# Attention and two expert layers on one core: the load of q, and where its transposes are copied

## The chip, the cores and the metric

The kernel runs on one core of one Trainium2 chip. The metric is the device time of one execution in microseconds. A core has engines that each take their own instructions in the order of the program: TensorE (PE) multiplies, and its weight loads are shown apart (PEld); VectorE (DVE), ScalarE (ACT) and GpSimd (POOL) do elementwise work; SyncE (SP) issues the DMAs here. PE writes to PSUM, the other engines copy from there to SBUF.

## The reference, cut

Attention without softmax comes first, with 8 batches of 8 heads, 576 positions and 64 columns, then two layers of two matmuls each:

```python
def _attn_ref(q, k, v, g_norm):                    # each [8, 8, 576, 64]
    kv = np.einsum('bhsd,bhse->bhde', k, v)
    out = np.einsum('bhsd,bhde->bhse', q, kv)
    rms = np.sqrt(np.mean(out * out, axis=-1, keepdims=True) + 1e-06)
    return (out / rms * g_norm).astype(np.float32)
...
    x = np.ascontiguousarray(attn_out.transpose(0, 2, 1, 3)).reshape(B * S, H * D)   # [4608, 512]
    x = _moe_ref(x=x, **moe_kwargs)       # h = x @ w_in [512, 2048]; max(0.01 h, h) @ w_out [2048, 512]
    return _moe2_ref(x=x, **moe2_kwargs)  # h = x @ w_in [512, 2048]; (h - tanh h) @ w_out [2048, 512]
```

q, k, v and the output are fp32; the four weight matrices come as fp64.

## The kernel before

**The big matmuls.** Each matmul of the two layers is cut into two by two blocks and done with seven products of sums of blocks in place of eight of blocks. Each product is taken from fp16 high and low parts of both operands, in PE instructions of 128x288 (L637). ACT and DVE make the high and low parts of the activations (tiles opa and ops, L574 and L581), POOL and DVE the sums of blocks (L614). A product's result goes from PSUM (ps_a to ps_d) to an SBUF tile u or c by ACT (L694) and is added to the layer's result g by DVE (L705); ACT applies the activation (L1258), and g is stored to DRAM by SP (L784).

**The weights.** A block of a weight matrix comes in as pairs of 32-bit words (L415) and is made into fp32 w1f (L429 on ACT, L433 to L473 on DVE, L496 and L500 on POOL). A maximum over the weights (mw, L465; m_w, L360; most_w, L331) gives a scale, s1g at L375. With it ACT writes the high part (L516) and DVE the low part (L519) of a block w_0, w_1, ... The first layer's columns use w_0 to w_7 in turn.

**Attention.** A batch goes in four pairs of heads; `load_pair` loads k, v and q of one pair. Positions are cut in a way that partition p holds the six positions 6p to 6p+5, so CP = 96 partitions and NC = 6 chunks. k and v come in one DMA each, with 6x64 values in a row of DRAM per partition and head. q comes in two DMAs, one for each head, into a tile laid out as chunk, head, column, in pieces of 64 values. In `pair`, step kv multiplies k by v (L962, PSUM tile pk), and ACT copies the two heads' 64x64 blocks to the diagonal of kvd (L973). Step qtr(r) transposes three chunks of both heads by three PE instructions to one PSUM bank pq (L982); ACT copies its 128x288 to qt[r] (L990), where 64 partitions hold one head and 64 the other. Step o(r) multiplies kvd by qt[r] (L998, PSUM tile po), so o(0) needs the first copy and o(1) the second. ACT squares po (L1004), and ACT (first batch) or DVE (L1013) copies it to xg. Step m sums the squares (L1035, pm); root and reciprocal of this are iv (L1057, L1065). For the first batch PE spreads iv over the partitions (pb, L1102) and DVE multiplies xg by it (L1108); for later batches iv goes through DRAM to a tile bc (L1074) and POOL multiplies (L1080).

**Order.** Class Plan sets the order of all instructions in one run through the program, from durations and delays written by hand: each step is put into the time line of its engine where it fits, and the order of the planned times is the order of the program. A step's planned time thus moves other engines' steps around it. Loads stand on SP in planned order too: in the first 48 us k, v and q of a pair and then four blocks of words; there are never more than eight loads under way, and an issue beyond that waits. The first batch's pairs run before the first product; three pairs of the second batch follow between its first products, and each later pair is spread over products of the stream, its steps kv, qtr(0), qtr(1), o(0), o(1), m at offsets 1, 4, 6, 8, 10 and 13 products. At the end `store` writes the output rows.

Of the kernel before, what the change touches and what calls it, by code (L numbers as in the profile page):

```python
# [11 lines left out]
F32 = mybir.dt.float32  # L12
I32 = mybir.dt.int32
AF = mybir.ActivationFunctionType
# [16 lines left out]
P = 128  # L31
# [170 lines left out]
@with_exitstack  # L202
def body(ctx, tc, *args):
    q, out, w1 = args[0], args[-1], args[4]
    sizes = (*q.shape, *out.shape, w1.shape[1])
    pools = {
        "const": ctx.enter_context(tc.tile_pool(name="const", bufs=1)),
        "wpool": ctx.enter_context(tc.tile_pool(name="wpool", bufs=1)),
        "work": ctx.enter_context(tc.tile_pool(name="work", bufs=1)),
        "dram": ctx.enter_context(tc.tile_pool(name="dram", bufs=1, space=DRAM)),  # L210
        "ps": ctx.enter_context(tc.tile_pool(name="ps", bufs=1, space=PSUM)),
    }
    delays = {}
    unseen = Unseen()
    while True:
        late = lay_out(Plan(delays, True), unseen, {n: unseen for n in pools}, sizes, [unseen] * len(args))
        if late is None:
            break
        delays[late[0]] = delays.get(late[0], 0.0) + late[1]
    with tc.manual_schedule():  # L220
        lay_out(Plan(delays, False), tc.nc, pools, sizes, args)


def lay_out(plan, nc, pools, sizes, args):
    q, k, v, g_norm, w1, w2, w3, w4, out = args
    B, H, S, D, NT, DM, DFF = sizes
    NP = DFF // P // 2
    CP = 96
    NC = S // CP
    T1 = S // 2  # L230
# [9 lines left out]
    L, M, X = (Slots(work, kind, n) for kind, n in (("l", NL), ("m", NM), ("x", NX)))  # L240
# [4 lines left out]
    def bank(n, name):  # L245
        if n in used:
            plan.miss(("bank", n))
        used.add(n)
        return ps.tile([P, 512], F32, tag=f"p{n}", name=name)

    def free(n):
        used.discard(n)
        plan.met(("bank", n))
# [31 lines left out]
    ident = const.tile([P, P], F32, name="ident")  # L285
# [641 lines left out]
    def att_bank(name):  # L927
        n = next(n for n in ATT if n not in used and n != att_n[0])
        att_n[0] = n
        return bank(n, name), n  # L930
# [3 lines left out]

    def load_pair(b, c, held):
        for nm, src in (("k", k), ("v", v), ("q", q)):
            apart = nm != "q"
            held[nm] = L.take([CP, 2, NC, D] if apart else [CP, NC, 2, D], F32, nm)
            if apart:
                nc.sync.dma_start(  # L940
                    out=held[nm].ap.rearrange("p h c d -> p h (c d)"),
                    in_=src[b, 2 * c:2 * c + 2].rearrange("h (p c) d -> p h (c d)", p=CP),
                )
                continue
            for h in range(2):
                nc.sync.dma_start(out=held[nm].ap[:, :, h], in_=src[b, 2 * c + h].rearrange("(p c) d -> p c d", p=CP))

    kv_n = [0]

    def two_heads(t, a):  # L950
        return t.ap[:, a].rearrange("p h d -> p (h d)")

    def pair(b, c, held):

        kk, n = c % 2, c // 2
        qt, sq, po = {}, {}, {}
# [19 lines left out]
                L.give(held["v"])  # L976
            plan.do("A", e + 0.15, 0.5, go)

        def qtr(r):
            qt[r] = att_bank("pq")  # L980
            for a in range(NC // 2):
                nc.tensor.transpose(  # L982
                    qt[r][0][:, CP * a:CP * a + CP], two_heads(held["q"], r * NC // 2 + a), ident[:CP, :CP]
                )

        def q_after(r, e):
            def go():
                src, n_ = qt[r]
                qt[r] = X.take([P, T1], F32, "qt")
                nc.scalar.activation(out=qt[r].ap, in_=src[:, :T1], func=AF.Copy)  # L990
                free(n_)
                if r == 1:
                    L.give(held["q"])
            plan.do("A", e + 0.15, 0.42, go)

        def o(r):
            po[r], po[r, 0] = att_bank("po")
# [161 lines left out]
    t = 1.0  # L1159
# [7 lines left out]
    for o in order:  # L1167
        if o[0] == "a":
            held = {}
            at(t, lambda o=o, held=held: load_pair(o[1], o[2], held))  # L1170
            ta[o[1:]] = (t + 6.5, held)
            t += 3.4
        else:
            later = after_scale.setdefault(o[1:], []) if o[1] in LATE else None
            convert(0, o[1], o[2], t, 5.5, place_w1(o[1], o[2]), later, sums_first(*o[1:]) if o[1] in SOON else [])
            t += 1.7
# [38 lines left out]
    for hp in range(4):  # L1215
        c = PAIRS[hp]
        t_, held = ta[0, c]
# [16 lines left out]
    for b in range(1, B):  # L1234
        for hp in range(4):
            c = PAIRS[hp]
# [3 lines left out]
            held = ta[b, c][1] if (b, c) in ta else {}  # L1240
# [4 lines left out]
    for n, b, c, held in loads:  # L1245
        extra.setdefault(max(n, 0), []).insert(0, (0.0, lambda b=b, c=c, held=held: load_pair(b, c, held), None))
# [199 lines left out]
    e = c3 + 20.0  # L1446
# [6 lines left out]
    def store(t, col0, d0, n):  # L1453

        r = 0
        while r < P:
            b, rest = divmod(col0 + r, S)
            c, p0 = divmod(rest, CP)
            m = min(P - r, CP - p0)
            nc.sync.dma_start(out=out_view[b, c, p0:p0 + m, d0:d0 + n], in_=t[r:r + m, :])  # L1460
            r += m
# [59 lines left out]
```

## Time and profile before

| | us |
|---|---|
| time, median of 3 runs | 1518.28 (1515.27 to 1518.82) |
| time of the profiled execution | 1520.94 |
| span of the profiled execution | 1519.1 |
| PE busy in it | 1452.1 |
| DVE, ACT, POOL busy | 1249.7, 903.6, 673.5 |

The profiled execution is one run that the profiler recorded; its span goes from the first to the last instruction, and its time is 1.8 us longer. An engine's rows have the start of an instruction, its duration, the engine, the line, the operation, the tile written and the tiles read. What stands in brackets behind a row is the time in which the engine stood idle before it, and the instruction or DMA that ended the idle time. Start to start, instructions of an engine lie a little closer than their durations say, since one begins before the one ahead has ended. The granted clock PEclk is a share of 2.4 GHz.

### The profile page before, as it was taken

The page shows a single profiled execution, that of the slowest core. Times are in us where ns is not written, and L with a number is a line of the kernel's source. Part 1 is how long each engine was busy: PE and PEld are TensorE (multiplying, and loading weights), DVE is VectorE, ACT ScalarE, POOL GpSimd, SP SyncE. Part 2 cuts the span into 40 slices and gives each one's busy share as a digit, 9 for nine tenths or more (in the row PEclk, how much of TensorE's full clock was granted, in tenths as well). Part 3 has the DMA queues.
Part 4 walks back from the last instruction along what each step waited for, and adds up shares of the span by engine and source line. Part 5 has one row for each costly group of instructions (what it writes and reads, how often), then busy time and mean ns, then how long its engine had stood idle before and what let it go on. Part 6 is the DMA issues. An engine that isn't in the chain of part 4 may idle for free. (4 is left out here: it accounts for less than half of the span.)

```text
span 1519.1 us, 32831 instructions
## 1 busy us (share of the span) xinstructions
PE 1452.1 (96%) x12674; PEld 1198.8 (79%) x12674; DVE 1249.7 (82%) x1971; ACT 903.6 (59%) x1461; POOL 673.5 (44%) x636
## 2 busy tenths in 40 slices
PE   6589899999999999999999999999998999999998
PEld 3367677776777777777777888888887888888887
DVE  5796677777877899999996888978999988888871
ACT  4477666667767645444442677778877554445540
POOL 3142330353642455445442355458876543444430
PEclk9799999999999999999999999999999999999999
DMA  9937999999977845655555865546668744444431
GB/s 247 205 97 215 260 277 268 265 284 312 325 275 278 333 146 192 202 161 193 186 169 192 318 224 205 210 173 231 244 232 303 248 144 151 144 146 146 142 96 35
DMA packets 187693, 321.82 MB, mean 212 GB/s; under 512 B 54033, under 2 KB 129681, under 8 KB 187537
## 3 DMA queue, kind: packets, MB, share of 16 engines
q1 hardware_dynamic: 187536, 319.73, 66.1%
q8 instruction: 99, 1.62, 0.4%
q14 instruction: 58, 0.47, 0.1%
HBM read 189.66 MB, written 130.01 MB: 210 GB/s over the span
## 5 line engine op out<-in xcount | busy, mean ns | idle before, releaser
L637 PEld LDWEIGHTS <-w 128*128 128x128 f16 x8400 | 821.0, 98 | 218.3 <-issue 42.8
L614 POOL TENSOR_TENSOR gl<-gl 128x256 f32<-128x256 f32 (+1 forms) x272 | 299.5, 1102 | 365.2 <-DVE gl L614 140.1
L637 PE MATMUL ps_a<-ops,w 128*128 128x288 f16 (+1 forms) x2400 | 332.9, 282 | 13.2 <-DVE ops L581 4.8
L637 PE MATMUL ps_c<-ops,w 128*128 128x288 f16 (+1 forms) x2352 | 316.7, 283 | 18.6 <-DVE g L705 18.6
L637 PE MATMUL ps_a<-opa,w 128*128 128x288 f16 (+1 forms) x2016 | 283.8, 281 | 0.1
L637 PEld LDWEIGHTS <-ops 128*128 128x128 f16 x1728 | 169.1, 98 | 20.8 <-issue 1.3
L637 PE MATMUL ps_b<-opa,w 128*128 128x288 f16 (+1 forms) x1200 | 176.0, 283 | 0.0
L614 DVE TENSOR_TENSOR gl<-gl 128x256 f32<-128x256 f32 (+1 forms) x272 | 151.9, 560 | 4.7
L1424 POOL TENSOR_TENSOR g<-g,th 128x512 f32<-128x512 f32 x72 | 113.7, 1579 | 92.9 <-ACT th L1421 85.5
L637 PEld LDWEIGHTS <-opa 128*128 128x128 f16 x1296 | 127.1, 98 | 15.0
L574 ACT ACTIVATE ops<-gl 128x1152 f16<-128x1152 f32 x64 | 74.4, 1162 | 96.5 <-POOL gl L614 96.2
L583 DVE SCALAR_TENSOR_TENSOR ops<-gl,inv,ops 128x1024 f16<-128x1024 f32 x72 | 103.2, 1433 | 29.5 <-ACT ops L576 29.3
L576 ACT ACTIVATE ops<-gl,inv 128x1024 f16<-128x1024 f32 x72 | 82.4, 1144 | 58.5 <-POOL gl L614 58.3
L1080 POOL TENSOR_TENSOR xg<-xg,bc 128x1152 f32<-128x1152 f32 x14 | 37.7, 2694 | 140.3 <-DMA bc<-iv 108.4
L696 ACT ACTIVATE u<-ps_a,up 128x256 f32<-128x256 f32 x144 | 67.9, 472 | 53.5 <-PE ps_a L637 50.0
L705 DVE SCALAR_TENSOR_TENSOR g<-ps_c,u 128x288 f32<-128x288 f32 x128 | 57.8, 452 | 50.7 <-PE ps_c L637 50.1
L581 DVE TENSOR_TENSOR ops<-gl,ops 128x1152 f16<-128x1152 f32 x64 | 93.8, 1470 | 6.2 <-ACT ops L574 6.2
L637 PE MATMUL ps_c<-w,ops 128*128 128x256 f16 x864 | 97.3, 273 | 0.2 <-DVE osb L705 0.2
L637 PE MATMUL ps_a<-w,ops 128*128 128x256 f16 x864 | 95.8, 273 | 0.7 <-ACT c L696 0.7
L614 POOL TENSOR_TENSOR x1g<-x1g 128x256 f32<-128x256 f32 x72 | 66.1, 920 | 48.6 <-DVE opa L583 45.3
L581 DVE TENSOR_TENSOR opa<-gl,opa 128x864 f16<-128x864 f32 x64 | 79.9, 1249 | 3.7 <-ACT opa L574 3.3
L583 DVE SCALAR_TENSOR_TENSOR opa<-gl,inv,opa 128x768 f16<-128x768 f32 x72 | 80.2, 1115 | 0.1
(133 smaller groups left out, 2139.0 us busy)
## 6 DMA issues: line engine op xcount, KB each, us to landing
g<-g SPq DMA_DIRECT2D x64, 576.0 KB, 6.1
gl<-g SPq DMA_DIRECT2D x64, 576.0 KB, 4.5
g<-g SPq DMA_DIRECT2D x72, 512.0 KB, 3.3
gl<-g SPq DMA_DIRECT2D x72, 512.0 KB, 4.3
wd<-wo SPq DMA_DIRECT2D x48, 448.0 KB, 3.4
w<-wd SPq DMA_DIRECT2D x24, 896.0 KB, 7.1
words<-in_moe_w_in_dram SPq DMA_DIRECT2D x64, 256.0 KB, 6.9
words<-in_moe_w_out_dram SPq DMA_DIRECT2D x64, 256.0 KB, 4.7
```

Source lines behind the costliest of these rows:

```text
L574: nc.scalar.activation(out=o, in_=i_, func=AF.Copy)
L576: nc.scalar.activation(out=o, in_=i_, func=AF.Identity, scale=scale())
L581: nc.vector.tensor_tensor(out=o, in0=i_, in1=h, op=ALU.subtract)
L583: nc.vector.scalar_tensor_tensor(out=o, in0=i_, scalar=scale(), in1=h, op0=ALU.mult, op1=ALU.subtract)
L614: lambda: e.tensor_tensor(out=g()[:, o], in0=g()[:, a], in1=g()[:, b], op=op),
L637: nc.tensor.matmul(out=out_, lhsT=a, rhs=c, start=start and m == 0, stop=stop and m == n - 1, skip_group_check=not fresh,)
L696: nc.scalar.activation(out=t, in_=src, func=AF.Identity, scale=self.scale)
L705: nc.vector.scalar_tensor_tensor(out=o, in0=src, scalar=self.minus if sub else self.scale, in1=t, op0=ALU.mult, op1=ALU.add,)
L1080: e.tensor_tensor(out=x, in0=x, in1=held[kk].ap[:, n0:n1], op=ALU.mult)
L1424: e.tensor_tensor(out=g()[:, n], in0=g()[:, n], in1=held["t"].ap[:, n], op=ALU.subtract)
```

## The change

q is loaded as k and v are, in one DMA with 6x64 values in a row. Step qtr takes a head h in place of half of the chunks: each of its three PE instructions transposes two neighbouring chunks of that head together, so partitions 0 to 63 of PSUM hold the even chunks and 64 to 127 the odd ones. Two ACT copies of 64x288 follow: the PSUM half r goes to the head's half of qt[r]. A pair so has four copies in place of two, planned at 0.41 us each, and o(0) needs the first and the third of them, o(1) the second and the fourth. qt[0] now holds chunks 0, 2, 4 and qt[1] chunks 1, 3, 5, and `store` maps the output rows to match. Lines behind the edit carry numbers that are three to eight lower.

```diff
     def load_pair(b, c, held):
         for nm, src in (("k", k), ("v", v), ("q", q)):
-            apart = nm != "q"
-            held[nm] = L.take([CP, 2, NC, D] if apart else [CP, NC, 2, D], F32, nm)
-            if apart:
-                nc.sync.dma_start(
-                    out=held[nm].ap.rearrange("p h c d -> p h (c d)"),
-                    in_=src[b, 2 * c:2 * c + 2].rearrange("h (p c) d -> p h (c d)", p=CP),
-                )
-                continue
-            for h in range(2):
-                nc.sync.dma_start(out=held[nm].ap[:, :, h], in_=src[b, 2 * c + h].rearrange("(p c) d -> p c d", p=CP))
+            held[nm] = L.take([CP, 2, NC, D], F32, nm)
+            nc.sync.dma_start(
+                out=held[nm].ap.rearrange("p h c d -> p h (c d)"),
+                in_=src[b, 2 * c:2 * c + 2].rearrange("h (p c) d -> p h (c d)", p=CP),
+            )
...
-        def qtr(r):
-            qt[r] = att_bank("pq")
+        def qtr(h):
+            held["pq", h] = att_bank("pq")
             for a in range(NC // 2):
                 nc.tensor.transpose(
-                    qt[r][0][:, CP * a:CP * a + CP], two_heads(held["q"], r * NC // 2 + a), ident[:CP, :CP]
+                    held["pq", h][0][:, CP * a:CP * a + CP],
+                    held["q"].ap[:, h, 2 * a:2 * a + 2].rearrange("p c d -> p (c d)"), ident[:CP, :CP],
                 )
 
-        def q_after(r, e):
-            def go():
-                src, n_ = qt[r]
-                qt[r] = X.take([P, T1], F32, "qt")
-                nc.scalar.activation(out=qt[r].ap, in_=src[:, :T1], func=AF.Copy)
-                free(n_)
+        def q_after(h, e):
+            def go(r):
+                src, n_ = held["pq", h]
+                if r not in qt:
+                    qt[r] = X.take([P, T1], F32, "qt")
+                nc.scalar.activation(
+                    out=qt[r].ap[D * h:D * h + D], in_=src[D * r:D * r + D, :T1], func=AF.Copy
+                )
                 if r == 1:
-                    L.give(held["q"])
-            plan.do("A", e + 0.15, 0.42, go)
+                    free(n_)
+                    if h == 1:
+                        L.give(held["q"])
+            plan.do("A", plan.do("A", e + 0.15, 0.41, lambda: go(0)), 0.41, lambda: go(1))
...
-            c, p0 = divmod(rest, CP)
+            n_, p0 = divmod(rest, CP)
+            c = 2 * n_ - (NC - 1) * (2 * n_ // NC)
```

The plan's order moves with the edit. On DVE, from the first batch's scaling to the maximum of the first weights (m_w): L1108 (L1105 after) multiplies xg by the spread norm, L1013 (L1010) copies a pair's output of the second batch, the others convert words. Before:

```order
L1108 TENSOR_TENSOR xg<-xg,pb 128x288
L465 TENSOR_REDUCE mw<-words 128x1
L452 SCALAR_TENSOR_TENSOR w1f_615<-words,w1f_615 128x512
L1108 TENSOR_TENSOR xg<-xg,pb 128x288
L465 TENSOR_REDUCE mw<-words 128x1
L1013 COPY xg<-po 128x288
L360 TENSOR_REDUCE m_w_727<-mw 128x1
```

and after:

```order
L465 TENSOR_REDUCE mw<-words 128x1
L1010 COPY xg<-po 128x288
L446 SCALAR_TENSOR_TENSOR w1f_615<-words,w1f_615 128x512
L1010 COPY xg<-po 128x288
L452 SCALAR_TENSOR_TENSOR w1f_615<-words,w1f_615 128x512
L1105 TENSOR_TENSOR xg<-xg,pb 128x288 x4
L452 SCALAR_TENSOR_TENSOR w1f_615<-words,w1f_615 128x512
L1105 TENSOR_TENSOR xg<-xg,pb 128x288
L360 TENSOR_REDUCE m_w_778<-mw 128x1
```

Between the last maximum over words (mw) and m_w there now stand two copies, three conversions and five multiplications, where one copy stood.

Also on DVE, ahead of the first product that uses w_5: L519 makes the low parts of w_5 and w_6, L705 adds products to g, L446 and L452 convert words. Before:

```order
L705 SCALAR_TENSOR_TENSOR g<-ps_c,u_1133 128x288
L519 SCALAR_TENSOR_TENSOR w_5_1125<-w1f_933,s1g,w_5_1125 128x896
L1013 COPY xg<-po 128x288
L452 SCALAR_TENSOR_TENSOR w1f_1068<-words,w1f_1068 128x512
L705 SCALAR_TENSOR_TENSOR g<-ps_c,u_1296 128x288
L519 SCALAR_TENSOR_TENSOR w_5_1125<-w1f_943,s1g,w_5_1125 128x896
L705 SCALAR_TENSOR_TENSOR g<-ps_b,c_1277 128x288
L519 SCALAR_TENSOR_TENSOR w_6_1242<-w1f_951,s1g,w_6_1242 128x896
L705 SCALAR_TENSOR_TENSOR g<-ps_c,u_1234 128x288
```

and after:

```order
L705 SCALAR_TENSOR_TENSOR g<-ps_b,c_1263 128x288
L473 TENSOR_SCALAR w1f_1159<-w1f_1159 128x512
L446 SCALAR_TENSOR_TENSOR w1f_1159<-words,w1f_1159 128x512
L440 TENSOR_SCALAR w1f_1160<-w1f_1160 128x512
L452 SCALAR_TENSOR_TENSOR w1f_1159<-words,w1f_1159 128x512
L705 SCALAR_TENSOR_TENSOR g<-ps_c,u_1224 128x288
L446 SCALAR_TENSOR_TENSOR w1f_1160<-words,w1f_1160 128x512
L519 SCALAR_TENSOR_TENSOR w_5_1185<-w1f_941,s1g,w_5_1185 128x896
L452 SCALAR_TENSOR_TENSOR w1f_1160<-words,w1f_1160 128x512
L519 SCALAR_TENSOR_TENSOR w_5_1185<-w1f_976,s1g,w_5_1185 128x896
L519 SCALAR_TENSOR_TENSOR w_6_1344<-w1f_1062,s1g,w_6_1344 128x896
```

The add of u_1224 is the one of u_1234 before, that of the last product with w_3, and PE's next product is the first with w_5; both low parts of w_5 now stand behind this add.

On ACT, one of the first pairs that are spread over products: L990 (L984) copies transposes, L694 copies products, L1004 (L1001) squares po. Before:

```order
L990 ACTIVATE qt<-pq 128x288
L694 ACTIVATE c_1682<-ps_a 128x288
L694 ACTIVATE u_1688<-ps_a 128x288
L990 ACTIVATE qt<-pq 128x288
L1258 ACTIVATE g<-g 128x1152
L1004 ACTIVATE sq<-po 128x288
```

and after:

```order
L984 ACTIVATE qt<-pq 64x288 x2
L694 ACTIVATE c_1694<-ps_a 128x288
L694 ACTIVATE u_1700<-ps_a 128x288
L984 ACTIVATE qt<-pq 64x288 x2
L1255 ACTIVATE g<-g 128x1152
L1001 ACTIVATE sq<-po 128x288
```

Two copies stand where one stood, and the rest of the order is the same.

## Rows read from the trace of the kernel before

**Rows 1.** the page, part 1: busy time, share of the span, instructions.

```profile
PE 1452.1 (96%) x12674; PEld 1198.8 (79%) x12674; DVE 1249.7 (82%) x1971; ACT 903.6 (59%) x1461; POOL 673.5 (44%) x636
```

**Rows 2.** waits of PE: line waited for, us in total, times, longest.

```profile
PE ps_c L637 <- DVE g L705: 18.6, 16, 3.0
PE pk L962 <- DMA v<-in_v_dram: 15.4, 6, 6.7
```

**Rows 3.** timeline of PE, the last wait of the start.

```profile
80.56 0.64 PE L637 MATMUL ps_a<-ops,w 128*128 128x288 f16 x2 [2.65 <-DVE ops L581]
```

**Rows 4.** timeline of PE, 164 to 177 us.

```profile
168.42 0.90 PE L637 MATMUL ps_a<-ops,w 128*128 128x288 f16 x6 [3.12 <-ACT u L694]
172.27 1.60 PE L637 MATMUL ps_c<-ops,w 128*128 128x288 f16 x6 [2.71 <-DVE g L705]
```

**Rows 5.** timeline of SP, the loads of one pair, and the next k.

```profile
14.53 0.60 SPq L940 DMA_DIRECT2D k<-in_k_dram  x1
16.04 1.32 SPq L946 DMA_DIRECT2D q<-in_q_dram  x2
17.40 4.86 SPq L415 DMA_DIRECT2D words<-in_moe_w_in_dram  x4
22.30 0.60 SPq L940 DMA_DIRECT2D k<-in_k_dram  x1
```

**Rows 6.** windows: busy time by engine, then clock, DMA share, GB/s; words alone.

```profile
32.00:39.00 7.00, 5.35 (x27) 2.54 (x23) 4.51 (x11) 5.33 (x12) 2.81 (x5) 1.00 1.09 347
```

**Rows 7.** DMA view, 14 to 32 us: GB/s in 40 equal slices.

```profile
GB/s 203 202 228 313 332 346 344 358 337 203 208 242 213 197 214 191 207 211 205 231 319 339 332 351 359 295 217 208 215 225 217 233 171 190 207 180 221 250 290 300
```

**Rows 8.** timeline of DVE: first batch's reciprocal, and the first weight scale.

```profile
46.41 1.94 DVE L1065 RECIPROCAL iv<-iv 128x288 f32<-128x288 f32 x1
63.48 0.15 DVE L375 TENSOR_TENSOR s1g<-s_w,gcol 128x1 f32<-128x1 f32 x1
```

**Rows 9.** timelines of DVE around w_5, and of PE at its first use.

```profile
103.69 1.14 DVE L519 SCALAR_TENSOR_TENSOR w<-w1f,s1g,w 128x896 f16<-128x896 f32 x1
105.11 0.68 DVE L452 SCALAR_TENSOR_TENSOR w1f<-words,w1f 128x512 int32<-128x512 int32 x1
105.71 0.45 DVE L705 SCALAR_TENSOR_TENSOR g<-ps_c,u 128x288 f32<-128x288 f32 x1
106.08 1.66 DVE L519 SCALAR_TENSOR_TENSOR w<-w1f,s1g,w 128x896 f16<-128x896 f32 x1
109.47 0.46 DVE L705 SCALAR_TENSOR_TENSOR g<-ps_c,u 128x288 f32<-128x288 f32 x1 [0.30 <-PE ps_c L637]
...
109.27 0.90 PE L637 MATMUL ps_a<-opa,w 128*128 128x288 f16 x6
```

**Rows 10.** windows (columns as in rows 6), behind the wait at 168 us.

```profile
170.00:177.00 7.00, 4.73 (x21) 3.15 (x21) 6.96 (x11) 4.23 (x8) 5.26 (x5) 0.51 0.75 225
```

**Rows 11.** timelines of SP and POOL, third batch: q's issues, the multiplication by bc.

```profile
153.41 1.37 SPq L946 DMA_DIRECT2D q<-in_q_dram  x2
...
164.50 2.61 POOL L1080 TENSOR_TENSOR xg<-xg,bc 128x1152 f32<-128x1152 f32 x1 [6.75 <-DMA bc<-iv]
```

**Rows 12.** timeline of PE: two later waits in the stream.

```profile
354.44 1.60 PE L637 MATMUL ps_c<-ops,w 128*128 128x288 f16 x6 [1.51 <-DVE g L705]
...
394.41 0.92 PE L962 MATMUL pk<-v,k 96*64 96x64 f32 x24 [1.42 <-DMA v<-in_v_dram]
```

**Rows 13.** groups of ACT by form, 100 to 450 us: busy, mean ns, idle.

```profile
L990 ACT ACTIVATE qt<-pq 128x288 f32<-128x288 f32 x47 | 19.1, 405 | 6.0 <-PE pq L982 6.0
L973 ACT ACTIVATE kvd<-pk 64x64 f32<-64x64 f32 x46 | 9.9, 216 | 7.3 <-PE pk L962 6.9
```

**Rows 14.** timelines of ACT and PE, a streamed pair: second copy, first product.

```profile
99.94 0.41 ACT L990 ACTIVATE qt<-pq 128x288 f32<-128x288 f32 x1 [0.33 <-PE pq L982]
...
101.22 0.65 PE L998 MATMUL po<-qt,kvd 128*128 128x288 f32 x2
```

**Rows 15.** timeline of ACT: the latest copy of the stream's pairs.

```profile
343.51 0.39 ACT L990 ACTIVATE qt<-pq 128x288 f32<-128x288 f32 x1
```

More of the change, by code (lines that the diff above doesn't have):

```diff
@@ L936, in load_pair @@
         for nm, src in (("k", k), ("v", v), ("q", q)):
-            apart = nm != "q"
-            held[nm] = L.take([CP, 2, NC, D] if apart else [CP, NC, 2, D], F32, nm)
-            if apart:
-                nc.sync.dma_start(
-                    out=held[nm].ap.rearrange("p h c d -> p h (c d)"),
-                    in_=src[b, 2 * c:2 * c + 2].rearrange("h (p c) d -> p h (c d)", p=CP),
-                )
-                continue
-            for h in range(2):
-                nc.sync.dma_start(out=held[nm].ap[:, :, h], in_=src[b, 2 * c + h].rearrange("(p c) d -> p c d", p=CP))
+            held[nm] = L.take([CP, 2, NC, D], F32, nm)
[3 more added lines that the diff above has]
+            )
     kv_n = [0]
-    def two_heads(t, a):
-        return t.ap[:, a].rearrange("p h d -> p (h d)")
     def pair(b, c, held):
```

## The prediction, made before the changed kernel was run

> **What bounds the kernel now.** I read the page first. TensorE (PE) is busy for 1452.1 of 1519.1 us [rows 1], and the changed kernel gives it the same matmuls and six transposes per pair of heads as before. So the change can move the time by the 67 us in which PE stands, by PE's clock, and by nothing else. The waits by engine say what PE stands for [rows 2]: 18.6 us for the sums that VectorE (DVE) adds, 15.4 us for v of the attention pairs. PE's times then place them: most of its waits lie before 80.56 us, where the last of the start ends after 2.65 us [rows 3], and the longest later stretch with waits begins at 168.42 us [rows 4]. I therefore take four places apart: the start, the first columns after it, the stalls in the stream, and the transposes themselves.
>
> **Start: q in long rows.** Until 48 us the load queue is the limit: SyncE issues k, v, two halves of q and four blocks of weight words per pair and is held up at the words. From one k to the next it takes 7.8 us (14.53 to 22.30) [rows 5]. A pair brings 0.885 MB of k, v, q and 1.049 MB of words. Words alone move at 347 GB/s [rows 6]; at this rate the 1.93 MB would take 5.6 us. The 2.2 us above that is the most that q's 256-byte rows can cost. The least: the rate falls to about 211 GB/s in the slices with k, v and q and is near 340 between them [rows 7]. If k and v stay at the low rate and q alone rises to 347, its 0.295 MB fall from 1.40 to 0.85 us, a gain of 0.55. Nothing in the slices sets q apart from k and v, which had long rows already, yet q has two transfers and six times as many rows. I take 1.3 us per pair, near the middle.
>
> Four pairs of the first batch stand ahead of the reciprocal at 46.41 us [rows 8], so it comes 5.2 us earlier (2.2 to 8.8). The weight scale s1g at 63.48 gains less: the changed order puts five multiplications, three conversions and a copy more ahead of its maximum on DVE, some 4 us of work of which a part fills DVE's waits; I take half of the gain, 2.6. DVE then makes the operands of the first products ahead of weight splits that stood before them now (two of 1.14 us [rows 9] ahead of the last), and the last operand wait, which ends at 80.56 [rows 3], should so end about 5.3 us earlier. **Start: -5.3** (-2.5 to -8).
>
> **The first columns: a weight that comes late.** The order on DVE shows a cost there. Now the two splits of w_5 run at 103.69 and 106.08, and the second is done at 107.74, 1.5 us before PE needs it at 109.27. The next add, at 109.47, waits for the product just before [rows 9]. In the changed order both splits stand behind that add, with two steps of weight conversion among them. From start to start the rows have 0.37 for an add and 0.60 for a conversion, 0.08 less than they last. So 109.47 plus an add (0.37), a conversion (0.60), a split (1.14 less 0.08), a conversion (0.60) and a split to its end (1.14) gives 113.24. PE could do three matmuls with the first half (0.37), so it stands 3.6 us. DVE can't go ahead: it takes its instructions in the order shown. **+3.6.** After a wait of 3.12 us in the stream the clock was 0.51 for 7 us with 4.73 us of work [rows 4, 10], that is about 1.2 instead of 2.4 GHz, which cost 2.4 us. I take the same here: **+2.4** (0 to 3.4).
>
> **The stall at 168 us.** The third batch's row scales bc are issued right behind q's 153.41, land so late that GpSimd (POOL) waited 6.75 us for them to 164.50, and PE's wait of 3.12 us follows through the operand made from them [rows 4, 11]. The change puts one issue of q in place of two: a k took 0.60 to issue where q's two took 1.32 [rows 5], so SyncE saves some 0.7 us here too, of 1.37 [rows 11], and the transfer some 0.5 to 1.3. Part of the gain is eaten by what is queued beside it: **-1.4** (0 to -5.8 if both waits at 168 and 172 vanish, and 2.4 more if the clock stays up).
>
> **The other stalls in the stream.** One wait for v, 1.42 us at 394.41, ends at a transfer behind q's of the pairs before [rows 12]; with half of q's rate penalty gone I count it out: **-1.4** (0 to -1.9 with a smaller one before it). The wait at 354.44 (1.51 us, with a half clock behind it) [rows 12] comes from an operand behind a stored tile; queues are emptier by a transfer or two: **-1.0** (0 to -3.5).
>
> **The copies.** Before, one ScalarE (ACT) copy of 128x288 filled one qt, 0.405 us each [rows 13]. Now a copy fills 64 of 128 partitions; a copy of half as many partitions with the same 288 columns is nowhere in the trace. The nearest are this one (0.405) and the copy of 64x64 (0.216) [rows 13]. The half copy shares its columns with the first and its partitions with the second; I take 0.41, by the columns, and 0.22 as the low end. 64 more copies are 26 us of ACT, which is busy for 59% of the span [rows 1], so ACT is not the bound. What counts is the order: out product 0 now needs the third copy, the first of the second head, and not the first alone. The transposes of the second part end about 0.03 before ACT takes up the copy at 99.94 and the product starts at 101.22 [rows 14]: ACT may answer 0.86 us late before PE waits. In the 24 pairs of the stream the copy after the second transposes came later than this in three: by 2.04 us at 343.51, where ACT stood behind a weight split that had waited for POOL [rows 15], and by about 0.2 at two others. **+2.4** (0 to +14, the second rival). In the first batch the four copies stand one behind the other ahead of the product; two more of them cost PE 0.6 to 0.8 us per pair, covered by the wait for the next v there, since PE is idle until it comes. If loads get fast enough to remove that cover, that is the price for each of the four pairs. The stores of the last stage are as many as before, to other rows of the output; I cost them at nothing, as they are off PE's path, and 0.5 at worst if the last one is slower.
>
> **Sum.** -5.3 + 3.6 + 2.4 - 1.4 - 1.4 - 1.0 + 2.4 = -0.7 us against the profiled execution. That one took 1520.94, its span 1519.1 and 1.8 around it, and so lies 2.66 above the median of the runs, 1518.28. 1520.94 - 0.7 = 1520.2, less 2.66 is **1517.6**. The bound of a measurement is 0.3%, 4.55 us: faster means below 1513.7, slower above 1522.8. The forecast is thus no change that can be told, with the gain of the loads spent at w_5.
>
> **Rivals.** First, *the loads gain the whole 2.2 us and the stalls go*. Start -8.0, w_5 +3.6 with no loss of clock, the stall at 168 gone with its half clock (-8.2), v -1.9, 354 -2.5, copies +2.4: -14.6, that is 1503.7. For it speaks that words alone reach 347 GB/s and that the stall hangs on a DMA of the queue which gets shorter; against it that k and v in long rows show the low rate as well. Half-way cases lie about 1510.
>
> Second, *ACT becomes the gate of the out products*. Place: the third copy before each first out product; it decides from 0.86 us after the second transposes on. If the added copies, which now also stand in front of the u and c copies of the main products, make ACT late by 0.6 more than its slack in half of the 24 pairs, PE waits 7.2 us, and if three of these waits drop the clock (2.4 each, as in the row of the half clock) 7.2 more: +14.4 in place of +2.4, so 1529.6. For it: ACT's copies come in clumps, and three pairs exceed the slack already. Against it: most of them start 0.15 us after the transposes.
>
> Third, *long rows don't do what they should*: the low rate in the slices belongs to k, v and q alike, whatever the row. Then the start gains nothing, w_5 still costs 3.6 and 2.4, the copies 2.4, and the stall at 168 gives back its 0.7 of issue: +7.7, that is 1526.0. For it speaks that the slices with k and v are as slow as those with q [rows 7]; against it that the stretch of words alone, in long rows, has nearly twice their rate [rows 6]. The Trainium skill's page "DMA: Bandwidth & Descriptors", section "Why small descriptors are slow (HBM only)", gives a packet about 3 cycles above its 32-byte beats, which makes 11 cycles of 256 B. By that (an estimate from the page) q's 66 cycles for six rows become 51, some 0.3 us per pair, and the rival would be off by 1.2. The fall from 347 to about 211 GB/s is larger than that rule gives.
>
> **How the numbers follow.** Forecast .45 (from 1513 to 1522; .38 of it within the bound, .05 faster, .02 slower). First rival .27, all faster, spread from 1503.7 to 1513. Second .15, third .13, both slower. So faster .32, same .38, slower .30. For 8 in 10 I leave out the far half of the second rival and the far third of the first: 1507 to 1528.
>
> **What would show it.** Right: 32 issues of q with 288 KB, the reciprocal about 5 us earlier; a wait of 3 to 4 us for w in the first product of the fifth column, a clock near 0.5 behind it; the stall after the third batch's scales shorter, not gone. The first rival shows as no stall at all there, and a reciprocal 8 us earlier; the second as many waits of out products for the ACT copy of qt, the third as an unchanged distance between two loads of k. I would be wrong most simply if w_5 were in time, or if some other operand were to wait in its place.

## The result, and the profile after

The changed kernel takes 1530.25 us (median, 1522.61 to 1539.89) where the kernel before takes 1517.7 beside it: a ratio of 1.009, with a 95% interval of 1.0065 to 1.0115. It is slower, by 12.6 us between the medians, and outside the range of 1507 to 1528 that was given. Its executions also differ more from each other than those of before (1515.27 to 1519.44). Its profiled execution took 1535.21, 14.3 more than that of before.

The page of the changed kernel, to be read against [rows 1]:

```profile
span 1533.4 us, 32882 instructions
PE 1453.1 (95%) x12674; PEld 1198.9 (78%) x12674; DVE 1252.5 (82%) x1971; ACT 930.0 (61%) x1525; POOL 671.1 (44%) x636
```

PE has the work that it had (1453.1 against 1452.1); ACT has 64 more instructions and 26.4 us more, as worked out. The span is 14.3 us longer, so what was added is PE's waiting, and the clock. The waits of PE by releaser (total us, times, longest), against [rows 2]:

```profile
PE pk L954 <- DMA v<-in_v_dram: 10.5, 3, 7.0
PE ps_a L637 <- ACT u L694: 10.3, 4, 5.2
PE ps_a L637 <- DVE w L519: 8.8, 3, 3.6
PE po L995 <- ACT qt L984: 5.6, 7, 1.1
PE ps_a L637 <- ACT w L516: 1.2, 1, 1.2
```

The waits for v fell from 15.4 to 10.5. That is not the faster load by itself: in the runs below the load alone has 15.1 us of these waits, and the copies with the old load have 10.1, since PE waits for half copies in their place. New are 8.8 and 1.2 us for w, the weights; 5.6 for qt, the half copies; and 6.9 more for u, against this row of before:

```profile
PE ps_a L637 <- ACT u L694: 3.4, 2, 3.1
```

Where on the line of time? The start of each PE instruction of L637 was set against that of the same instruction before (they come in the same order). The difference, in us, runs like this; a minus means that the changed kernel is ahead:

| place (us before) | what changes there | difference behind it |
|---|---|---|
| 84 | start: loads faster, half copies in the way | -3.7 |
| 109 to 123 | first product with w_5 | +8.4 |
| 168 to 323 | stall at bc | +9.4 |
| 323 to 358 | smaller waits gone, 354 with its half clock among them | +4.1 |
| 389 to 395 | wait for v gone | +3.6 |
| 397 to 400 | a new wait | +11.6 |
| 406 | a wait of before gone | +10.2 |
| 424 to 450 | longer waits for DVE's adds | +14.1 |
| the end | | +14.3 |

Two places make most of the loss: 12.1 us at w_5 and 8.0 near 397. A third, between 424 and 450, adds 3.9. PE's timeline at them, with the stall after the third batch's scales in its place:

```profile
106.94 0.42 PE L637 MATMUL ps_a<-opa,w 128*128 128x288 f16 x2 [1.17 <-ACT w L516]
110.93 0.90 PE L637 MATMUL ps_a<-opa,w 128*128 128x288 f16 x3 [3.56 <-DVE w L519]
115.47 0.42 PE L637 MATMUL ps_a<-opa,w 128*128 128x288 f16 x1 [3.65 <-DVE w L519]
...
177.69 0.90 PE L637 MATMUL ps_a<-ops,w 128*128 128x288 f16 x6 [3.95 <-ACT u L694]
...
405.76 1.60 PE L637 MATMUL ps_a<-ops,w 128*128 128x288 f16 x6 [5.24 <-ACT u L694]
...
459.14 1.60 PE L637 MATMUL ps_c<-ops,w 128*128 128x288 f16 x6 [2.58 <-DVE g L705]
```

The first three rows are the first product of w_5: 1.17 + 3.56 + 3.65 = 8.38 us, for ACT's high part and for DVE's two low parts. The fourth answers to [rows 4] and is 0.8 longer than it was. The fifth is new, and the last is 1.5 us longer than before.

The loads at the start did what was expected of them. SyncE's issues of k and words (SP), the 40 slices of GB/s from 14 to 32 us, and the reciprocal on DVE, for [rows 5, 7, 8]:

```profile
11.30 0.32 SPq L938 DMA_DIRECT2D k<-in_k_dram  x1
14.67 2.66 SPq L415 DMA_DIRECT2D words<-in_moe_w_in_dram  x4
17.96 0.32 SPq L938 DMA_DIRECT2D k<-in_k_dram  x1
...
GB/s 296 351 348 346 351 353 322 229 249 246 266 259 248 252 246 305 357 341 353 348 354 298 225 293 225 249 256 245 242 245 307 304 335 350 344 351 348 346 353 341
...
42.73 1.94 DVE L1062 RECIPROCAL iv<-iv 128x288 f32<-128x288 f32 x1
```

From one k to the next it is 6.7 us in place of 7.8, and the slices between the words now lie near 250 GB/s in place of 211. The reciprocal starts at 42.73, 3.7 us earlier.

### The profile page after: what moved, and what is told of

Its sections match the earlier page's. It is cut to its first block, busy times and chain, and to the rows that moved or that the text cites. A ratio compares the mean times of both kernels' runs of the same rounds, so it can differ in the third digit from the quotient of the medians.

```text
span 1533.4 us, 32882 instructions
## 1 busy us (share of the span) xinstructions
PE 1453.1 (95%) x12674; PEld 1198.9 (78%) x12674; DVE 1252.5 (82%) x1971; ACT 930.0 (61%) x1525; POOL 671.1 (44%) x636
## 5 line engine op out<-in xcount | busy, mean ns | idle before, releaser
L637 PEld LDWEIGHTS <-w 128*128 128x128 f16 x8400 | 822.4, 98 | 236.8 <-issue 48.3
L637 PE MATMUL ps_a<-ops,w 128*128 128x288 f16 (+1 forms) x2400 | 333.4, 283 | 17.2 <-ACT u L694 10.3
L637 PE MATMUL ps_c<-ops,w 128*128 128x288 f16 (+1 forms) x2352 | 317.3, 283 | 18.9 <-DVE g L705 18.7
L637 PE MATMUL ps_a<-opa,w 128*128 128x288 f16 (+1 forms) x2016 | 285.8, 282 | 10.1 <-DVE w L519 8.8
L637 PEld LDWEIGHTS <-ops 128*128 128x128 f16 x1728 | 169.1, 98 | 22.0 <-issue 2.5
L637 PE MATMUL ps_b<-opa,w 128*128 128x288 f16 (+1 forms) x1200 | 177.5, 285 | 0.0
L637 PEld LDWEIGHTS <-opa 128*128 128x128 f16 x1296 | 126.8, 98 | 14.7
L705 DVE SCALAR_TENSOR_TENSOR g<-ps_c,u 128x288 f32<-128x288 f32 x128 | 57.9, 452 | 49.6 <-PE ps_c L637 48.6
L637 PE MATMUL ps_a<-w,ops 128*128 128x256 f16 x864 | 95.8, 273 | 1.9 <-ACT c L696 1.9
L637 PE MATMUL ps_c<-w,ops 128*128 128x256 f16 x864 | 97.3, 273 | 0.2 <-DVE osb L705 0.2
```

The lines of the kernel that those rows point to most:

```text
L637: nc.tensor.matmul(out=out_, lhsT=a, rhs=c, start=start and m == 0, stop=stop and m == n - 1, skip_group_check=not fresh,)
L705: nc.vector.scalar_tensor_tensor(out=o, in0=src, scalar=self.minus if sub else self.scale, in1=t, op0=ALU.mult, op1=ALU.add,)
```

## What happens at w_5

The prediction read the order of DVE right and the time wrong. DVE and POOL of the changed kernel at that place, and behind them two windows (busy time by engine, then granted clock, DMA share, GB/s):

```profile
107.37 3.50 DVE L519 SCALAR_TENSOR_TENSOR w<-w1f,s1g,w 128x896 f16<-128x896 f32 x1
110.79 3.09 DVE L452 SCALAR_TENSOR_TENSOR w1f<-words,w1f 128x512 int32<-128x512 int32 x1
113.81 4.40 DVE L519 SCALAR_TENSOR_TENSOR w<-w1f,s1g,w 128x896 f16<-128x896 f32 x3
...
106.95 6.38 POOL L1077 TENSOR_TENSOR xg<-xg,bc 128x1152 f32<-128x1152 f32 x2 [1.36 <-ACT w L516]
...
111.00:115.50 4.50, 0.85 (x4) 0.24 (x5) 4.50 (x3) 0.00 (x0) 4.50 (x3) 0.50 0.85 226
115.50:122.00 6.50, 6.50 (x31) 4.52 (x32) 4.18 (x6) 3.90 (x7) 3.85 (x5) 0.58 0.02 4
```

The two splits of w_5 stand where the order shows them. But the first lasts 3.50 us where [rows 9] has 1.14, and the conversion behind it 3.09 where it had 0.68. From 106.95 to 113.3 GpSimd runs the second batch's two multiplications by bc: 6.6 us of DVE's time stand beside them, for 1.8 us of work. In the kernel before, they began only after both splits were done:

```profile
110.98 5.43 POOL L1080 TENSOR_TENSOR xg<-xg,bc 128x1152 f32<-128x1152 f32 x2 [1.49 <-ACT qt L990]
```

The windows behind the waits show about half the clock, 0.50 with 0.85 us of PE's work and 0.58 with 6.50. At the full clock that work takes 0.4 and 2.7 us less: most of the 3.7 us that the 12.1 have above the waits.

The trace of before has the same thing, where it cost nothing. An add and a conversion on DVE, and the multiplication on POOL beside them:

```profile
268.06 0.46 DVE L705 SCALAR_TENSOR_TENSOR g<-ps_b,c 128x288 f32<-128x288 f32 x1
268.43 3.11 DVE L446 SCALAR_TENSOR_TENSOR unit<-words,unit 128x512 int32<-128x512 int32 x1
...
268.36 2.63 POOL L1080 TENSOR_TENSOR xg<-xg,bc 128x1152 f32<-128x1152 f32 x1 [0.93 <-PE pq L982]
```

The add of 0.46 us begins shortly ahead; the conversion, 0.68 us alone, lasts 3.11: it ends 0.55 us after GpSimd's 2.63 are over. It is so for every conversion and split with two SBUF inputs that began more than 0.05 us behind such a multiplication and before its end, in this trace and in that of the changed kernel: a conversion ended 0.55 us behind the multiplication's end, a split 0.95 to 0.97. Those that began ahead of it kept their 0.68 and 1.14. The Trainium skill, page "SBUF — State Buffer", section "Who interferes with whom", states this as a rule: a VectorE instruction with two SBUF inputs and a GpSimd instruction that reads SBUF exclude each other for the whole of the instruction. The traces agree: what reads PSUM as one input (L705, L1013) keeps its 0.46 us beside GpSimd, what reads two SBUF tiles (L446, L519) does not when it begins second. A conversion with one SBUF input (L440, 0.43 us alone) didn't keep its time either: 1.35 to 2.62 us in the trace of before.

## Experiments

Each kernel was measured on one chip together with the kernel before, and its ratio is to that. Three kernels part load, copies and order. The plan's order follows from planned durations alone, so each can be changed without the others.

**The load alone**: the kernel before, with the changed `load_pair`, and

```diff
 def two_heads(t, a):
-    return t.ap[:, a].rearrange("p h d -> p (h d)")
+    return t.ap.rearrange("p h c d -> p (h c d)")[:, 2 * D * a:2 * D * a + 2 * D]
```

> The changed load alone: q in one DMA with rows of 1536 B. Transposes, copies and the order on TensorE, VectorE, ScalarE and GpSimd are those of before; since the transposes take q's tile as it lies, heads and chunks are mixed and the output is not the reference's. Theory O (the order that the plan made of the change costs the time, at w_5 above all): the gain of the start stays, first operand wait over 3 to 5 us earlier, no wait for w near 109 us, no half clock there; 3 to 6 us faster than before, about 1513. Theory C (more copies on ScalarE cost the time): the same here, so this run doesn't part O from C. Theory L (the long rows themselves make other transfers land late, as the operand that waited 8.6 us for a DMA near 404 us in the changed kernel): a stall of over 3 us in the stream that before doesn't have, 1520 or more.

Measured: 1512.83 us, ratio 0.9968 (0.9956 to 0.998), a gain of 4.9 us. PE at the end of the start, at the stall after bc, at the wait of 354 us and at a wait for v:

```profile
76.13 0.64 PE L637 MATMUL ps_a<-ops,w 128*128 128x288 f16 x2 [2.65 <-DVE ops L581]
...
163.51 0.90 PE L637 MATMUL ps_a<-ops,w 128*128 128x288 f16 x6 [2.59 <-ACT u L694]
...
348.56 0.90 PE L637 MATMUL ps_c<-ops,w 128*128 128x288 f16 x6 [0.86 <-DVE g L705]
...
389.07 0.92 PE L957 MATMUL pk<-v,k 96*64 96x64 f32 x24 [2.98 <-DMA v<-in_v_dram]
```

The start is 4.4 us earlier ([rows 3]), and of the stalls in the stream little is gained on balance: the one at 168 us is 0.5 shorter, the wait at 354 is 0.65 shorter and PE has its full clock behind it (1.00, against 0.57 before), which makes 2.3, and the wait for v at 394 is 1.6 longer than in [rows 12]. No new stall: theory L falls, and nearly all of the load's gain is what the start gives, 1.1 us per pair.

**Copies and order alone**, with the load of before: the changed kernel with the old `load_pair` and

```diff
-                    held["q"].ap[:, h, 2 * a:2 * a + 2].rearrange("p c d -> p (c d)"), ident[:CP, :CP],
+                    two_heads(held["q"], h * (NC // 2) + a), ident[:CP, :CP],
```

> The load of before (two DMAs per pair in 256-byte pieces) with the changed transposes, the four half copies and the changed order on all engines; q's tile is read in another order than it was loaded, so heads and chunks are mixed and the output is not the reference's. Theory O: the changed kernel without the gain of the start (3.7 us before w_5), so 1530 to 1536, with the waits for w_5 (over 7 us together) in the profile. Theory C: the same. Theory L: the stall near 404 us goes, about 1520 to 1525.

Measured: 1536.72 us, ratio 1.0121 (1.0108 to 1.0134). PE waits 8.22 us at w_5, and 5.79 at 407.79 for u, behind the same wait of ACT as below. Without the faster load the loss is larger.

**The changed kernel in the order of before**:

```diff
-            plan.do("A", plan.do("A", e + 0.15, 0.41, lambda: go(0)), 0.41, lambda: go(1))
+            plan.do("A", plan.do("A", e + 0.15, 0.21, lambda: go(0)), 0.21, lambda: go(1))
```

> The changed kernel with each half copy planned at 0.21 us in place of 0.41: the plan then gives TensorE, VectorE and GpSimd the order of before, row for row, and ScalarE too, but for two half copies in each copy's place. All the work of the changed kernel is in it. Theory O: no wait at w_5 and no half clock there; the start 3 to 5 us earlier than before, some 1 to 4 us of waits of out products for the half copies in the stream: 1513 to 1519. Theory C: ScalarE's 26 us more cost the same as in the changed kernel, 1527 or more. Theory L: as in the first run, with a new stall in the stream, 1520 or more.

Measured: 1518.66 us, ratio 1.0001 (0.9991 to 1.0011). It does all the work of the changed kernel and is as fast as before. So by these ratios the load gives 4.9 us, the half copies take 5.0, and the order that the plan makes of 0.41 us takes the rest, 10.6 to 13.5 (the changed kernel was measured twice, at 1.0071 below and at 1.009). The 4.9 and 5.0 belong to the order of before; in the changed order the load gives 4.7 to 7.6 by the ratios, and what the copies take there was not measured. Theory O holds for the larger part and C for 5 us. PE's waits for the copies at the start, with ACT beside one of them, the one wait in the stream, and two of SyncE's issues of k:

```profile
19.37 2.29 PE L995 MATMUL po<-qt,kvd 128*128 128x288 f32 x4 [1.28 <-ACT qt L984]
27.30 1.24 PE L995 MATMUL po<-qt,kvd 128*128 128x288 f32 x4 [1.40 <-ACT qt L984]
...
17.52 0.82 ACT L984 ACTIVATE qt<-pq 64x288 f32<-64x288 f32 x2 [0.23 <-PE pq L974]
18.24 0.65 ACT L429 ACTIVATE w1f<-words 128x512 f32<-128x512 f32 x1
18.91 0.83 ACT L984 ACTIVATE qt<-pq 64x288 f32<-64x288 f32 x2
...
345.01 0.75 PE L995 MATMUL po<-qt,kvd 128*128 128x288 f32 x2 [2.05 <-ACT qt L984]
...
13.06 0.32 SPq L938 DMA_DIRECT2D k<-in_k_dram  x1
20.88 0.32 SPq L938 DMA_DIRECT2D k<-in_k_dram  x1
```

In the first batch each first out product waits 0.9 to 1.4 us for its third copy, and ACT shows why: a conversion of words (L429) stands between the two pairs of copies. The first product of L637 starts at 72.71 where the load alone has 66.42. Not all of these 6.3 us need be the copies': from one k to the next it is 7.8 us in this execution, as with short rows, where the load alone has 6.5 (11.04 to 17.57) and the changed kernel 6.7. Why the long rows were no faster here is open, and with it where the 5.0 us stand. In the stream the one long wait is 2.05 us, at the pair of [rows 15], where 2.04 was forecast.

**Who holds up DVE at w_5.** GpSimd's multiplication for the second batch was left out in one kernel:

```diff
-            e.tensor_tensor(out=x, in0=x, in1=held[kk].ap[:, n0:n1], op=ALU.mult)
+            if b != 1:
+                e.tensor_tensor(out=x, in0=x, in1=held[kk].ap[:, n0:n1], op=ALU.mult)
```

> The changed kernel, leaving out GpSimd's two multiplications of the second batch by its row scales (so that batch's rows are not normed); the order of all else is unchanged. They ran beside VectorE's split of w_5 and the conversion behind it, which lasted 3.50 and 3.09 us. Theory P (VectorE's instructions that read two SBUF operands stand while such a GpSimd instruction runs, and this made 3.6 us of expected wait into 8.4): the split lasts about 1.14 and the conversion 0.68, TensorE's waits for w_5 fall from 8.4 to about 4, and the time by 4 to 7 us, to 1523 to 1526. Rival Q (the split lasts long because of its own operands or a late DMA): durations and time unchanged within 2 us.

Measured: 1528.84 us, ratio 1.007 (1.0057 to 1.0083). DVE and PE at w_5:

```profile
107.00 1.14 DVE L519 SCALAR_TENSOR_TENSOR w<-w1f,s1g,w 128x896 f16<-128x896 f32 x1
108.06 0.68 DVE L452 SCALAR_TENSOR_TENSOR w1f<-words,w1f 128x512 int32<-128x512 int32 x1
108.66 3.94 DVE L519 SCALAR_TENSOR_TENSOR w<-w1f,s1g,w 128x896 f16<-128x896 f32 x3
...
106.18 0.42 PE L637 MATMUL ps_a<-opa,w 128*128 128x288 f16 x2 [1.17 <-ACT w L516]
108.19 0.54 PE L637 MATMUL ps_a<-opa,w 128*128 128x288 f16 x3 [1.59 <-DVE w L519]
109.86 0.42 PE L637 MATMUL ps_a<-opa,w 128*128 128x288 f16 x1 [1.12 <-DVE w L519]
```

The split is back at 1.14 and the conversion at 0.68, and PE waits 1.17 + 1.59 + 1.12 = 3.88 us in place of 8.38: P holds at the place, and 3.6 was close for the order by itself. With the clock, PE falls back by 6.2 us at w_5 in place of 12.1. The whole gained little, and the 4 to 7 us that P forecast did not come: the profiled execution is 8.4 us shorter than the changed kernel's, but it is the fastest of its runs, and the ratio of 1.007 is that of the changed kernel's second measurement (1.0071). What took the local gain back in the other runs is not settled.

In another kernel all of these multiplications were cut in four:

```diff
-            x = xg[b, kk].ap[:, n0:n1]
-            e.tensor_tensor(out=x, in0=x, in1=held[kk].ap[:, n0:n1], op=ALU.mult)
+            for m_ in range(n0, n1):
+                e.tensor_tensor(
+                    out=xg[b, kk].ap[:, m_:m_ + 1], in0=xg[b, kk].ap[:, m_:m_ + 1], in1=held[kk].ap[:, m_:m_ + 1],
+                    op=ALU.mult,
+                )
```

> The changed kernel with each of GpSimd's multiplications by the row scales (128x1152) cut into four instructions of 128x288, in the same place of the order. Theory P1 (VectorE waits for the end of the one GpSimd instruction that runs): the split of w_5 and the conversion behind it get in between the pieces and last at most 0.7 us longer than alone, so the waits for w_5 fall from 8.4 to 5 or 6 us and the time by 3 to 5. Rival P2 (VectorE gets no turn as long as GpSimd has work of this kind queued): the split lasts 3 us as before, the time within 2 us.

Measured: 1524.51 us, ratio 1.0035 (1.0022 to 1.0048), against 1.0071 of the changed kernel on the same chip: 5.5 us faster by the ratios. DVE and PE at w_5:

```profile
106.25 1.68 DVE L519 SCALAR_TENSOR_TENSOR w<-w1f,s1g,w 128x896 f16<-128x896 f32 x1
107.86 1.28 DVE L452 SCALAR_TENSOR_TENSOR w1f<-words,w1f 128x512 int32<-128x512 int32 x1
...
105.83 0.42 PE L637 MATMUL ps_a<-opa,w 128*128 128x288 f16 x2 [1.17 <-ACT w L516]
107.99 0.54 PE L637 MATMUL ps_a<-opa,w 128*128 128x288 f16 x3 [1.74 <-DVE w L519]
110.80 0.42 PE L637 MATMUL ps_a<-opa,w 128*128 128x288 f16 x1 [2.27 <-DVE w L519]
```

The split lasts 1.68, the conversion 1.28, PE waits 5.18 us. DVE gets its turn between the pieces: P1 holds, P2 falls. At w_5 PE now falls back by 8.6 us, where the two profiles of the changed kernel have 12.1 and 11.0; so only 2.4 to 3.5 of the 5.5 us stand there, and where the rest comes from was not followed up.

**The stall near 397 us.** The changed kernel once more:

> The changed kernel once more, as the measure for the three beside it on the same chip. Expected 1526 to 1534. If the stall near 404 us belongs to the order that the plan made (theory S), it is in this profile too, 4 to 6 us before the product there; if it was a chance of that one execution (rival), it is not.

Measured: 1530.92 us, ratio 1.0071 (1.0058 to 1.0084). ACT's operand opa in the first measurement of the changed kernel (the cause of its last PE row above):

```profile
404.49 0.92 ACT L574 ACTIVATE opa<-xg 128x864 f16<-128x864 f32 x1 [8.56 <-DMA wd<-wo]
```

and ACT and PE in this one:

```profile
401.80 0.92 ACT L574 ACTIVATE opa<-xg 128x864 f16<-128x864 f32 x1 [10.48 <-DMA wd<-wo]
...
403.07 1.36 PE L637 MATMUL ps_a<-ops,w 128*128 128x288 f16 x5 [5.91 <-ACT u L694]
```

The operand's place was that of a split weight whose store to DRAM (wd) was still under way. It waited 8.2 to 10.5 us in each of five profiled executions with the changed order (this one, the first, and those with the old load, without and with cut multiplications), and in none of six with the order of before on VectorE. So it belongs to the order. The third place does too: between 424 and 450 us PE falls back by 2.8 to 5.0 us against the trace of before in these five, and gains 0.6 to 1.5 in the five other kernels with the order of before. No run was made for that place. Then the tile's place was given back later:

```diff
-            place.give(held["o"])
+            plan.at(plan.now + 10.0, lambda: place.give(held["o"]))
```

> The changed kernel, in which the tile of a split weight of the later layers is given back 10 us later than its store is issued, so that no operand gets the place while the store still reads it; the order moves a little with it (some 40 of 1800 rows on VectorE), w_5 not. Theory S (the wait of 8.56 us of the operand opa for the store of wd at 404 us is the plan handing out a place too early, and costs 5.2 us and a half clock behind): no such wait, 5 to 8 us faster than the changed kernel, 1521 to 1526. Rival: the wait was a chance of one execution, or another takes its place; within 2 us.

Measured: 1529.72 us, ratio 1.0064 (1.0051 to 1.0078): no change that can be told from the changed kernel. DVE, ACT and PE there:

```profile
390.83 0.46 DVE L705 SCALAR_TENSOR_TENSOR g<-ps_b,c 128x288 f32<-128x288 f32 x1 [6.59 <-POOL xg L1077]
...
398.77 0.92 ACT L574 ACTIVATE opa<-xg 128x864 f16<-128x864 f32 x1 [1.57 <-DMA wd<-wo]
...
396.75 0.64 PE L637 MATMUL ps_c<-ops,w 128*128 128x288 f16 x2 [7.78 <-DVE g L705]
```

The wait for the store fell to 1.57, but an add on DVE now waits 6.59 us for a place that GpSimd's late multiplication holds, and PE 7.78 for that. The rival was right: another wait took its place. That the first wait alone costs the 8.0 us is thus not shown; only that the order near there hands out places before the work that holds them is over, in both kernels.

**A better version?** The first batch's second copies went to VectorE, in the kernel planned at 0.21:

```diff
-                nc.scalar.activation(
-                    out=qt[r].ap[D * h:D * h + D], in_=src[D * r:D * r + D, :T1], func=AF.Copy
-                )
+                to, from_ = qt[r].ap[D * h:D * h + D], src[D * r:D * r + D, :T1]
+                if b == 0 and r == 1:
+                    nc.vector.tensor_copy(out=to, in_=from_)
+                else:
+                    nc.scalar.activation(out=to, in_=from_, func=AF.Copy)
```

> The kernel planned as before (half copies planned at 0.21 us), where the first batch's two copies for the second qt go to VectorE in place of ScalarE. It has the order of before but for these eight copies. In the kernel with all four on ScalarE, out products at the start waited 0.9 to 1.4 us each for them and the first product came 6.3 us later than with the load alone. Theory C1 (that start is where the copies cost, by ScalarE's queue): the first product 3 to 5 us earlier than there, 1513 to 1516. Rival C2 (the copies only move to a queue that is just as full): within 1.5 us of 1518.7.

Measured: 1516.48 us, ratio 0.9986 (0.997 to 1.0002). PE's first product of L637:

```profile
69.72 0.90 PE L637 MATMUL ps_a<-opa,w 128*128 128x288 f16 x6
```

It starts 3.0 us earlier than with all copies on ACT, and the first batch's out products still wait 0.5 to 0.9 us each. That is at the edge of C1's range for the start, but the loads ran faster in this execution too (6.8 us from one k to the next, for 7.8), so the copies' share of the 3.0 is not shown. The time lies between what C1 and C2 forecast, and the 2.3 us that the ratios differ by are within the noise. What is left of the price may be the dependence itself, two copies ahead of an out product where there was one; no run parts that from the rest.

The kernel before with GpSimd's multiplications in four pieces (the edit above):

> The kernel before with each of GpSimd's multiplications by the row scales cut into four instructions of 128x288; nothing else. In its trace VectorE's conversions and splits beside such a multiplication last 2.3 to 3.1 us in place of 0.7 to 1.1 in about ten places, mostly with slack ahead of TensorE. Theory P1: those durations fall below 1.9 and TensorE's smaller waits for VectorE's adds shrink, 0 to 4 us faster. Rival: the cuts cost GpSimd more than VectorE gains (four starts in place of one), 0 to 2 us slower.

Measured: 1518.23 us, ratio 1.0005 (0.9991 to 1.002). No change, though the instructions got shorter: beside these multiplications the six longest splits and conversions lasted 2.28 to 3.11 us before and none is above 1.69 now. In this order TensorE seems to have lost nothing by them.

Both edits together, in long rows and in the order of before:

> The long rows with half copies planned at 0.21 us, the first batch's second copies on VectorE, and GpSimd's multiplications in four pieces: the version that the runs so far point to. 1512 to 1516, if the gains of the load (5.1 us), less what is left of the copies (about 3), and of the pieces (0 to 4) add up; within 2 us of 1516.5 if the pieces give nothing in this order.

Measured: 1516.98 us, ratio 0.9999 (0.9987 to 1.0012). The pieces add nothing here. None of the versions that compute the whole is clearly faster than before; of the load's 4.9 us the half copies take most.

## Why the prediction was wrong, point by point

- **Start, -5.3.** Right in kind; the load alone gave -4.4 at the same wait, 1.1 per pair for 1.3. In the changed kernel 3.1 to 3.7 were left. The prediction named the price of four half copies, "0.6 to 0.8 us per pair", and left it out since the wait for v covers it. That held in part: the out products of the four pairs waited 0.7 to 0.9 each, and the waits for the next v shrank in exchange, but behind the fourth pair there is no next v, and the reciprocal came 0.9 later than with the load alone (42.73 for 41.86). The moved order had its own part in the start, as the prediction said of the first operands: with the copies and the old load that last wait ends at 77.97, 2.6 us earlier than before. These gains don't add up in the changed kernel.
- **w_5, +3.6 and +2.4.** This is the step that failed. The order was read rightly: with GpSimd's multiplications out of the way, the wait is 3.88 and the place costs 6.2 with the clock, as the 6.0 of the sum. But the durations were taken from [rows 9], where GpSimd does something else; in the changed order its multiplications by bc stand beside the splits, and the wait is 8.38, the half clock behind it 3.7: 12.1 in place of 6.0. The prediction compared the order of DVE alone at this place, not that of POOL. 1.17 of the wait is ACT's high part of w_5, which it did not look at either; the second low part comes last in any case. With 12.1 in place of 6.0 the sum would have come to 1523.7, so this is not the whole miss.
- **Stall at 168 us, -1.4, v, -1.4, and 354, -1.0.** The load alone gained 0.5 at 168 and 2.3 at 354, half clock included, and its wait for v grew by 1.6; its end is 5.1 us earlier and its start 4.4. So the in-stream gain of a faster load, 3.8 in the sum, was about 0.7 in all. The wait for v, in a queue of mixed transfers, did not shrink with the part of the queue that got shorter. In the changed kernel the stall at 168 grew by 0.8, while the wait for v at 394 and the one at 354 were gone.
- **Copies, +2.4.** A half copy has the mean of a whole one, as the groups of ACT in the changed kernel show against [rows 13]:

```profile
L984 ACT ACTIVATE qt<-pq 64x288 f32<-64x288 f32 x92 | 37.0, 402 | 6.4 <-PE pq L974 5.0
```

  The stream cost what was forecast in the order of before (one wait of 2.05). By the ratios the price in that order is 5.0 all the same; much of it seems to lie at the start, but how much is open, as said above.
- **What was not foreseen**: the wait near 397 us, +8.0, at a place handed out while a store still read it, and the 3.9 us between 424 and 450. The prediction compared orders at the start, at w_5 and on ACT; what the moved order does to the rest of the stream it put at nothing, and gave no reason. That the order as a whole costs 10.6 to 13.5 us is shown by the kernel planned at 0.21. How this is shared between w_5 and the stream is read from profiled executions alone: a repair at either place moved the waits but not, clearly, the time, except for the multiplications in pieces.
- **The rivals.** The first (loads) and the third (long rows without effect) fell with the load alone. The second, ACT as the gate in the stream, comes to the measured time (1529.6) by a way that isn't the kernel's: 5.6 us of waits for qt are there, but nearly all at the start. None of the rivals was the one that held: the moved order puts DVE's late splits beside the GpSimd work that blocks them, and makes new waits in the stream.

## What to carry to other kernels

Where a planner sets the order, a change of planned durations is a change of its own, and is measured by itself: here the same instructions planned at half the duration keep the old order and the old time. When an order moves a critical instruction, look at what the engines that it can block, or that block it, do beside it, and take its duration from a row with that neighbour. And the faster transfer was worth about what the stage bound by transfers gave; waits elsewhere that merely end at a DMA moved both ways and left 0.7 us.

## What the runs showed of the hardware

- A VectorE instruction with two SBUF inputs (0.68 or 1.14 us alone) lasted 2.3 to 3.5 us when it began behind a GpSimd multiplication of 128x1152 (2.6 to 3.3 us) and far from its end; with pieces of 128x288 the two at w_5 lasted 1.68 and 1.28. Adds and copies that read PSUM kept their 0.46.
- A ScalarE copy of 64x288 takes as long as one of 128x288 (402 and 405 ns).
- Three waits of 8.4 us in all at w_5 cost 12.1; 3.1 of the 3.7 us above the waits are the granted clock of 0.50 and 0.58, near the lower level of 1.2 GHz, in the 11 us from 111 on.
